# Attention and feed-forward layer on one core: the order of four engines written out in the source after the prologue, in place of the order of a rule-based planner

## The chip, the core and the metric

The kernel runs on one NeuronCore of a Trainium2 chip. The core has five engines with a queue each: TensorE (PE in the profile, its weight loads PEld), VectorE (DVE), ScalarE (ACT), GpSimd (POOL) and SyncE (SP), which here only issues transfers. Each engine works through its queue strictly in order, and the engines wait for one another through semaphores. The metric is the device time of one execution in microseconds (us): 689.67 us is the median of three runs of the kernel before (689.6 to 689.73).

## What is computed

The reference normalises an input `x` of 2048 rows by 640 columns, and adds three things: `x`, a multi-query attention with 32 heads of 20 columns each that share one key and one value head, and a feed-forward layer with 1728 hidden columns.

```python
q = (xn @ wq).reshape(B, S, 32, 20).transpose(0, 2, 1, 3)
k = xn @ wk                       # 2048 x 20, shared by all heads
v = xn @ wv                       # 2048 x 20
p = softmax(einsum("bhqd,bkd->bhqk", q, k) * 20 ** -0.5)
attn = einsum("bhqk,bkd->bhqd", p, v) ... @ wo
ffn = silu(xn @ w1) @ w2
out = x + attn + ffn
```

The bulk is the softmax: 32 heads x 2048 x 2048 exponentials.

## The kernel before, in words

**Tiling.** The queries are cut into four chunks of 512 and the heads into eight groups of four, which makes 32 groups; the keys into 16 tiles of 128. One score tile ("a head" below) is 128 keys x 512 queries of one head, and there are 32 x 16 x 4 = 2048 of them. A score matmul (`s_mm`, L1078) uses only 32 rows of the array, so matmuls of up to four different heads run at the same time in different rows; such a bundle is called a burst (`pe_set`, `joined`, L279). Each head fills one of PSUM's eight banks.

**Two ways for an exponential.** Most heads go to ScalarE: a set of two or three adjacent banks is read by one `exp` activation (L1166), and the result goes into slots of `Ebuf`; then one step of four matmuls per four heads multiplies with `v` (`make_pv_act`, L1201). The others go to VectorE in batches of four heads: `p1` (L1409) turns a score into the bit pattern of a bfloat16 power of two (one instruction per head, which also frees the bank), two shifts per batch make two more copies with other rounding (on GpSimd L1448, or on VectorE L1453), and three such matmul steps per batch, one per copy, form the weighted sum. A batch therefore costs TensorE two steps more than four heads on ScalarE do.

**Other work.** TensorE also runs the matmuls of `q`, of the hidden layer (`h`), of the output (`out`, and `y` for the last chunk), all through `col_mm` (L447). ScalarE has a `tanh` per hidden tile (L773), VectorE evicts all of these (L693, L776, L903, L919), copies each group's sums (L1250) and takes reciprocals (L851), and GpSimd normalises each group (L860). In some `out` and `y` steps the hidden matrix fills only half of the rows; such steps can be cut into single row matmuls (`row_mm`, L454) that ride in the free rows of a burst. The shifts and GpSimd's normalising (`op.port`) use a port that VectorE and GpSimd share; GpSimd waits by a semaphore for the last shift of VectorE that the plan put ahead (`calm`, L833), while VectorE's place relative to GpSimd is set by the planned order alone.

**What sets the order.** While the program is built, `build` plays through a schedule on the host (`Sched`, the main loop at the end of `build`). Each engine has a pool of operations, and rules choose the next one: `step_pe` (L1842) for TensorE, from the candidates of `pe_candidates` (L1730), and `step_other` (L1964) for the others by priority and earliest start. `plan` (L1084) chooses the banks of the next set: three adjacent ones or two. `dve_items` (L1362) chooses the head for VectorE, `dve_advance` (L1420) decides between GpSimd and VectorE for a shift, `take` (L1639) the bank of another job, `row_slice` (L1776) the row matmuls that fill a burst. The string `PLAN` varies the rules by stretch. Then `emit` (L2017) writes each engine's list out as its instruction stream with the semaphore waits that the data need. On the chip every engine's order is fixed; nothing is chosen at run time.

**Slots of Ebuf.** `e_slot` and `e_free` (L1119) give a set consecutive slots; a slot is free when all steps that use any part of the earlier set have been put into the order.

Of the kernel before, what the change touches and what calls it, by code (L numbers as in the profile page):

```python
# [15 lines left out]
D = 640  # L16
# [4 lines left out]
HG = 4  # L21
# [12 lines left out]
NJ = len(SHIFT)  # L34
# [77 lines left out]
def rule(n):  # L112
    return PLAN[n] if n < len(PLAN) else "a"
PACE = 1.0
ENDLEAD = 0.04
ENDFROM = 0.85

# [57 lines left out]
    return max(n / 2.4 + 3.0, 58.0)  # L175


class Job:


    def __init__(self, name, cost):
        self.name = name
        self.cost = cost
        self.bank = None
        self.mms = deque()
        self.consumers = []
        self.ready = None
        self.fixed = None
        self.head = None
        self.batch = None  # L190
        self.dyn = False
        self.issued = 0
        self.rest = {}
        self.burst = None
        self.row = None

    @property
    def done(self):
# [130 lines left out]
def build(nc, A_x, A_wq, A_wk, A_wv, A_wo, B_x, B_w1, B_w2, out, stack):  # L329
# [781 lines left out]
    def left_over(banks, gone):  # L1111

        left = set(banks).difference(gone)
        return sum(r <= left for r in RUN3)

    e_owner = [None] * NSLOT
    e_next = [0]

    def e_free(k):  # L1119
        return e_owner[k] is None or all(o is not None and o.done for o in e_users[e_owner[k]])  # L1120

    def e_slot(k):
        p = e_next[0] if e_next[0] + k <= NSLOT else 0
        return p if all(e_free(q) for q in range(p, p + k)) else None

    def make_s_act():
        n = att["n"]
        if n >= 2 and not exp_ops[n - 2].done:
            return None
        buf = plan(n)  # L1130
        if buf is None:
            return None
        items = next_items(len(buf), peek=True)
        if not items:
            return None
        buf = buf[:len(items)]
        pre = s_pre(items)
        if pre is None or not all(p.done for p in pre):
            return None
        es = e_slot(len(buf))  # L1140
        if es is None:
            return None

        def f(pe):
            ins = None
            for b, (g, kt, i) in zip(buf, items):
                ins = s_mm(pe, b, g, kt, i)
            return ins
        reads = [r for g in {it[0] for it in items} for r in q_res[g]] + [res("kT", kt) for kt in {it[1] for it in items}]
        wr = [sc.banks[b] for b in buf]  # L1150
        op = Op("pe", f, 216.0 + 4 * (len(items) - 1), pre=pre, reads=reads, writes=wr,
                mode="s", prio=0.0, name=f"S{n}", slots=frozenset(it[2] for it in items))
        op.run = buf

        def com(op, n=n, items=items, buf=buf, es=es):
            next_items(len(buf))
            e_next[0] = es + len(buf)
            for k in range(es, es + len(buf)):
                e_owner[k] = n
            att["n"] += 1  # L1160
            sc.free -= set(buf)
            w = len(items) * QW

            def ef(a):
                if len(buf) == 1 or buf[1] == buf[0] + 1:
                    return a.activation(Ebuf[:, es * QW:es * QW + w], ps[:, buf[0] * BANK:buf[0] * BANK + w], AF.Exp, scale=ESCALE)  # L1166
                src = ps[:, buf[0] * BANK:(buf[0] + 1) * BANK]
                return a.activation(Ebuf[:, es * QW:es * QW + w].rearrange("p (n q) -> p n q", q=QW),
                                    bass.AP(ps, src.offset, [list(src.ap[0]), [(buf[1] - buf[0]) * BANK, len(buf)], [1, QW]]), AF.Exp, scale=ESCALE)
            eo = act(ef, t_act(w) - 1.0, pre=[op], reads=[sc.banks[b] for b in buf], writes=[res("E", es + k) for k in range(len(buf))], prio=0.0,  # L1170
                     name=f"exp{n}")
            eo.on_commit = lambda op: sc.free.update(buf)
            exp_ops[n] = eo
            e_users[n] = []
            for j, (g, kt, i) in enumerate(items):
                d = pv_pend.setdefault((g, kt), {})
                d[i] = (es + j, eo, n)
                if len(d) == HG:
                    pv_queue[g].append(("a", kt, d))
                    po = make_pv_act(g, kt, d)  # L1180
                    for nn in {x[2] for x in d.values()}:
# [153 lines left out]
    def z_slot():  # L1335
        return next((k for k in range(min(ru.zcap, len(z_t))) if z_idle(k)), None)
# [80 lines left out]
    def pool_load():  # L1417
        return sc.t["pool"] - sc.t["pe"] + sum(o.occ for o in sc.pools["pool"])

    def dve_advance(job):  # L1420
# [14 lines left out]
        for j in range(1, NJ):  # L1435
            qk = XQ[j - 1]
            if qk is not None and len(s_last[j - 1]) == NW[j - 1] and len(xq_read[qk]) == DC + FC and all(o.done for o in xq_read[qk]):
                s_last[j - 1].append(sc.order["pe"][-1])
            wi = min(range(len(s_last[j - 1])), key=lambda k: -1 if s_last[j - 1][k] is None or k == NW[j - 1] and isinstance(s_last[j - 1][k], Op) else s_last[j - 1][k]["nth"])
            old = s_last[j - 1][wi]  # L1440
            s_last[j - 1][wi] = st
            lent = wi == NW[j - 1]
            t = xnT[:, 0:HG, qk * QW:(qk + 1) * QW] if lent else s_t[j - 1][wi][:, :]
            zin = z16.rearrange("p (h q) -> p h q", h=HG) if lent else z16
            r = res("s", j, wi)
            args = dict(pre=st["p1"] + ([idb] + [norm_op[n] for n in range(NT)] if old is None else [old] if isinstance(old, Op) else [old["pv"][j]]), reads=zr, writes=[r], name=f"s{j}")
            if j in POOL_J or pool_load() < ru.pj:
                op = pool(lambda v, t=t, j=j, zin=zin: v.tensor_scalar(t.bitcast(I16), zin, float(SHIFT[j]), 1.0, ALU.add, ALU.mult),  # L1448
                          POOL_SHIFT, POOL_END, prio=0.3, **args)
                op.port = True  # L1450
                op.gate = calm(op)
            else:
                op = dve(lambda v, t=t, j=j, zin=zin: v.tensor_scalar_add(t.bitcast(I16), zin, float(SHIFT[j])), t_dve(N, 4),  # L1453
                         prio=SPRIO - 0.01 * j, **args)
# [183 lines left out]

    def take(job, e):  # L1639
        b = job.fixed  # L1640
        if b is None:
# [175 lines left out]
    def xbanks():  # L1817
        return [b for b in sc.free if b in XBANKS] if pro else sc.free
# [100 lines left out]
    def fresh_u():  # L1919
        return att["pgroup"] < NGR and att["pgroup"] not in ubank  # L1920

    def commit_pe(e, op, what):
        if what[0] == "pv":
            if fresh_u():
                ok = [b for b in xbanks() if bank_at(b, "p") <= e + SLACK_B]
                b = min(ok, key=lambda b: (-left_over(sc.free, (b,)), -b)) if ok else min(xbanks(), key=bank_free_at)
# [51 lines left out]
    def finished():  # L1978
        return (att["pgroup"] >= NGR and not pro and not misc and not misc_front and cur_job[0] is None
                and all(not sc.pools[e] for e in sc.ENG))  # L1980

    idle = 0
    piece = 0
    while not finished():
# [7 lines left out]
        got = step_pe() if e == "pe" else step_other(e)  # L1992
        others = [sc.t[k] for k in sc.ENG if k != e]
        nxt = min(others)
        if got is None:
# [11 lines left out]
        idle = 0  # L2007
        if e == "pe":
            commit_pe(es, op, what)
        else:  # L2010
            sc.pools[e].remove(op)
            sc.commit(op, es)

    return sc, dma_sems, sem

# [158 lines left out]
```

## Time and profile before

| | |
|---|---|
| time, median of three runs | 689.67 us |
| span of the profiled execution | 688.3 us |
| TensorE busy, matmuls | 675.7 us (98%), 9821 |
| ScalarE busy | 666.4 us (97%), 728 instructions |
| VectorE busy | 591.3 us (86%), 1017 instructions |
| GpSimd busy | 581.7 us (85%), 349 instructions |
| transfers | 28.97 MB, mean 42 GB/s |

The profiled execution's span runs from its first to its last instruction; no separate time of that execution is given, so the 1.4 us between the span and the median are what lies around it. "Busy" is the union of the intervals in which instructions of the engine ran. Since matmuls overlap one another in the array and one activation overlaps the start of the next, a duration is longer than the distance from one start to the next; both are used below. A line "L1166" is a line of the kernel before.

### The profile page before, as it was taken

The numbers are of one execution on the slowest core, as the hardware profiler recorded it, in microseconds if no ns is written. First come the engines' busy times: TensorE is split into PE (matmuls) and PEld (weight loads), VectorE is DVE, ScalarE is ACT, GpSimd is POOL, SyncE is SP. The second block draws the span as 40 slices with busy tenths as digits, with TensorE's granted clock in tenths as the row PEclk, the third lists the DMA queues.
The fourth block names the chain that finished last, engine by engine and source line by source line (L and its number), as shares of the span: only waits on it lengthen the run. The fifth ranks groups of instructions, "written<-read, shape, count | busy, mean of one in ns | idle before, by whom it ended". The sixth has DMA issues, their size and how long they took to land.

```text
span 688.3 us, 22511 instructions
## 1 busy us (share of the span) xinstructions
PE 675.7 (98%) x9821; PEld 232.2 (34%) x9821; DVE 591.3 (86%) x1017; ACT 666.4 (97%) x728; POOL 581.7 (85%) x349
## 2 busy tenths in 40 slices
PE   8999999999999999999999999999999999999998
PEld 6432222222333333322323333332233333333345
DVE  7899988999989878798898897889999898987953
ACT  6999999999999999999999999999999999999992
POOL 6658899898988998899898889888889987879990
PEclk9999999999999999999999999999999999999999
DMA  8643220222221222422022222132222221223201
GB/s 226 190 160 42 19 23 14 35 34 25 23 29 12 32 38 29 72 36 30 9 22 30 29 31 33 26 37 61 31 22 20 21 27 23 32 20 70 23 7 41
DMA packets 34241, 28.97 MB, mean 42 GB/s; under 512 B 15486, under 2 KB 29662, under 8 KB 34142
## 3 DMA queue, kind: packets, MB, share of 16 engines
q1 hardware_dynamic: 33854, 27.20, 25.8%
q8 instruction: 77, 1.26, 0.8%
q10 hardware_dynamic: 288, 0.33, 0.1%
q14 instruction: 22, 0.18, 0.1%
HBM read 11.09 MB, written 2.62 MB: 20 GB/s over the span
## 4 chain that ended last, share of the span: by engine, by line
ACT 52%; PE 42%; DVE 3%; POOL 1%; DMA 0%; issue 0%; DVEq 0%; ACTq 0%
ACT sbt L1166 48%; PE psall L1201 14%; PE psall L1078 14%; PE psall L447 13%; ACT sbt L773 3%; DVE sbt L1409 2%; POOL sbt L1448 1%; PE psall L595 1%; PE psall L621 1%; DVE sbt L1453 0%; DMA sbt<-in_A_x_dram 0%; PE psall L999 0%; PE psall L1017 0%; ACT sbt L554 0%; DVE sbt L565 0%
## 5 line engine op out<-in xcount | busy, mean ns | idle before, releaser
L1166 ACT ACTIVATE sbt<-psall 128x1024 bf16<-128x1024 f32 (+1 forms) x656 | 640.0, 1138 | 3.2 <-PE psall L1078 3.0
L1448 POOL TENSOR_SCALAR sbt<-sbt 128x2048 int16<-128x2048 int16 x273 | 518.6, 1900 | 72.5 <-PE psall L1201 15.3
L1409 DVE TENSOR_SCALAR sbt<-psall 128x512 int16<-128x512 f32 x676 | 440.1, 685 | 63.1 <-PE psall L1078 58.0
L1078 PE MATMUL psall<-sbt 32*128 32x512 bf16 x2048 | 268.3, 384 | 3.3 <-ACT sbt L1166 2.0
L1201 PE MATMUL psall<-sbt 128*32 128x512 bf16 x3400 | 264.7, 384 | 1.9 <-POOL sbt L1448 0.6
L447 PE MATMUL psall<-sbt 128*32 128x320 bf16 (+2 forms) x3772 | 225.9, 332 | 2.1 <-DVE sbt L776 0.7
L1078 PEld LDWEIGHTS psall<-sbt 32*128 32x128 bf16 x2048 | 71.8, 91 | 236.9 <-ACT sbt L1166 174.1
L447 PEld LDWEIGHTS psall<-sbt 128*32 128x32 bf16 x3772 | 80.4, 95 | 85.5 <-issue 45.4
L1201 PEld LDWEIGHTS psall<-sbt 128*32 128x32 bf16 x3400 | 68.8, 94 | 115.5 <-issue 71.9
L1453 DVE TENSOR_SCALAR sbt<-sbt 128x2048 int16<-128x2048 int16 x65 | 47.6, 750 | 0.0
L860 POOL TENSOR_TENSOR sbt<-sbt 128x512 bf16<-128x512 f32 x30 | 38.3, 1277 | 4.9 <-DVE sbt L1453 2.7
L776 DVE SCALAR_TENSOR_TENSOR sbt<-sbt,psall 128x512 bf16<-128x512 bf16 x52 | 35.5, 682 | 3.8 <-ACT sbt L773 1.8
L773 ACT ACTIVATE sbt<-psall 128x512 bf16<-128x512 f32 x52 | 34.9, 671 | 0.2 <-PE psall L447 0.2
L454 PE MATMUL psall<-sbt 32*128 32x320 bf16 (+1 forms) x78 | 24.4, 313 | 0.0
L1250 DVE COPY sbt<-psall 128x512 f32<-128x512 f32 x31 | 21.2, 683 | 0.9 <-PE psall L1201 0.8
L919 DVE SCALAR_TENSOR_TENSOR sbt<-psall,sbt 128x320 f32<-128x320 f32 x8 | 3.9, 491 | 12.2 <-PE psall L447 7.0
L903 DVE SCALAR_TENSOR_TENSOR sbt<-psall,sbt 128x320 bf16<-128x320 f32 x24 | 11.6, 482 | 3.1 <-PE psall L447 1.7
L693 DVE TENSOR_SCALAR sbt<-psall 128x512 bf16<-128x512 f32 x20 | 13.5, 676 | 0.0
L572 POOL TENSOR_TENSOR sbt<-sbt 128x2 f32<-128x2 f32 x8 | 5.7, 710 | 8.5 <-DVE sbt L570 8.2
L1725 PE MATMUL psall<-sbt 128*32 128x256 bf16 (+1 forms) x188 | 11.1, 375 | 1.2 <-DVE sbt L487 1.2
L585 POOL TENSOR_SCALAR sbt<-sbt 128x640 bf16<-128x640 bf16 x12 | 10.4, 878 | 1.5 <-DVE sbt L577 1.5
L563 DVE BATCH_NORM_STATS2 sbt<-sbt 128x6 f32<-128x320 bf16 x14 | 6.6, 472 | 2.0 <-DMA sbt<-in_A_x_dram 2.0
(64 smaller groups left out, 118.3 us busy)
## 6 DMA issues: line engine op xcount, KB each, us to landing
sbt<-sbt SPq DMA_DIRECT2D x120, 64.0 KB, 3.8
sbt<-in_A_x_dram SPq DMA_DIRECT2D x28, 160.0 KB, 3.9
sbt<-sbt SPq DMA_DIRECT2D x213, 20.0 KB
out_dram<-sbt SPq DMA_DIRECT2D x14, 160.0 KB, 2.2
sbt<-in_B_w_dram SPq DMA_DIRECT2D x1, 2160.0 KB, 11.5
sbt<-in_B_w_dram SPq DMA_DIRECT2D x1, 2080.0 KB, 8.2
sbt<-sbt SPq DMA_DIRECT2D x75, 8.0 KB
sbt<-in_A_wq_dram SPq DMA_DIRECT2D x1, 800.0 KB, 6.7
```

Of the source, the lines that this page charges most:

```text
L447: ins = pe.matmul(ps[j * SLOT:(j + 1) * SLOT, b * BANK + off:b * BANK + off + n], w[:, j * SLOT:(j + 1) * SLOT], x, start=start, stop=stop ...
L454: return pe.matmul(ps[0:w.shape[-1], b * BANK:b * BANK + n], w[k], x[k], start=start, stop=stop, tile_position=(r * SLOT, 0))
L773: t = Op("act", lambda a: a.activation(t_buf[0:rows, ts, :], bk(job.bank, 0, QW, rows=rows), AF.Tanh, scale=0.5), t_act(512), ACT_END, pre ...
L776: u = Op("dve", lambda v: v.scalar_tensor_tensor(out=hT[par][0:rows, fk, :], in0=t_buf[0:rows, ts, :], scalar=1.0, in1=bk(job.bank, 0, QW, ...
L860: nm = pool(lambda e: e.tensor_tensor(oU[:, us, :], U_sb[:, us, :], Rrep, ALU.mult), 1356.0, POOL_END, pre=[uc] + lc + pack_op.get(divmod( ...
L1078: return pe.matmul(bk(b), kT_rep[i * SLOT:(i + 1) * SLOT, kt * P:(kt + 1) * P], qT[i * SLOT:(i + 1) * SLOT, g % NQ, :], start=True, stop=T ...
L1166: return a.activation(Ebuf[:, es * QW:es * QW + w], ps[:, buf[0] * BANK:buf[0] * BANK + w], AF.Exp, scale=ESCALE)
L1201: ins = pe.matmul(ps[i * SLOT:(i + 1) * SLOT, ub * BANK:ub * BANK + QW], lhsT, rhs, start=(first and k < HG), stop=(last and k >= len(lst) ...
L1250: return v.tensor_copy(U_sb[:, us, :], bk(ub))
L1409: p1 = Op("dve", lambda v: v.tensor_scalar(z16[:, i * QW:(i + 1) * QW], bk(job.bank), ZBIAS, 0.0, ALU.add, ALU.max), t_dve(QW) + 2.0, DVE_ ...
L1448: op = pool(lambda v, t=t, j=j, zin=zin: v.tensor_scalar(t.bitcast(I16), zin, float(SHIFT[j]), 1.0, ALU.add, ALU.mult), POOL_SHIFT, POOL_E ...
L1453: op = dve(lambda v, t=t, j=j, zin=zin: v.tensor_scalar_add(t.bitcast(I16), zin, float(SHIFT[j])), t_dve(N, 4), prio=SPRIO - 0.01 * j, **args)
```

## The change

Two strings are added. `ORDER` holds TensorE's order as tokens of three characters, 3046 of them; `OTHERS` holds the order of ScalarE, VectorE and GpSimd as one letter per operation, and under "port" the turns of GpSimd and VectorE on the shared port. Once TensorE's planned time has reached `HAND` (36 us), the prologue's jobs are done and no job is open, `follow` takes the next token in place of `step_pe`, and `follow_other` the next letter in place of `step_other`. SyncE's order stays with the rule. When the tokens run out, the rules go on.

A token `S20` is a set of two banks from bank 0 for ScalarE, `S14` a set of one bank, `D32` head 3 of the first open batch for VectorE into bank 2 (the first digit codes the batch, open or new, and the head), `E32` the same where the first of the batch's two shifts goes to VectorE instead of GpSimd, `a` and `d` a matmul step with `v` for heads of ScalarE or of VectorE, `n` the start of another job with its bank and `m` the next matmul step of that job. The small letter `s` (and `F`, `G`) starts a new burst where the capital would have joined the one before. There is no token for a single row matmul, and none for a filler.

The tokens and letters by count:

| | |
|---|---|
| sets for ScalarE: three banks, two banks, one bank | 69, 496, 56 (1255 heads) |
| heads for VectorE (D, E, F, G) | 705 |
| steps with `v`: a, d | 313, 518 |
| jobs begun: h, out, q, y | 54, 24, 18, 5 |
| further job steps m | 788 |
| ACT letters: exp, tanh | 621, 54 |
| DVE letters: p1, shifts, h, sums, out, q, y, other | 705, 116, 56, 30, 24, 18, 5, 3 |
| POOL letters: shifts, normalising | 234, 30 |

The rest of the diff: a slot of `Ebuf` becomes free as soon as the one step that reads it is in the order (`e_pv`); `make_s_act` takes the banks from the token, and for a token leaves out the rule that the exponential two sets before must be in the order; a job takes its bank from the token (`job.want`); the batch carries the choice of engine for its shift (`st["pool"]`).

```diff
+HAND = 36000.0
+ORDER = (
...
+OTHERS = {
+    "act": (
...
-    e_owner = [None] * NSLOT
+    e_pv = [FREE] * NSLOT
     def e_free(k):
-        return e_owner[k] is None or all(o is not None and o.done for o in e_users[e_owner[k]])
+        return e_pv[k] is not None and e_pv[k].done
...
-    def make_s_act():
+    def make_s_act(buf=None):
         n = att["n"]
-        if n >= 2 and not exp_ops[n - 2].done:
-            return None
-        buf = plan(n)
         if buf is None:
+            if n >= 2 and not exp_ops[n - 2].done:
+                return None
+            buf = plan(n)
+        if buf is None or not sc.free.issuperset(buf):
             return None
...
-            if j in POOL_J or pool_load() < ru.pj:
+            if j in POOL_J or st.get("pool", pool_load() < ru.pj):
...
+        if job.want is not None:
+            b = job.want
+            sc.free.remove(b)
...
+    def follow():
+        tok = ORDER[replay["at"]:replay["at"] + 3]
+        k, a, b = tok[0], tok[1], int(tok[2], 36)
+        if k in "sFG":
+            sc.pe_set = None
+            k = {"s": "S", "F": "D", "G": "E"}[k]
+        if k == "S":
+            op = make_s_act(tuple(range(b, b + int(a))))
+            what = ("s", None)
+        elif k in "DE":
...
+            dj.want = b
+            st["pool"] = k == "D"
+            op, what = dj.mms[0], ("dj", dj)
+        elif k in "ad":
...
+        elif k == "m":
+            op, what = cur_job[0].mms[0], ("mm", None)
+        elif k == "n":
...
+    def follow_other(e):
+        t = sc.t[e]
+        todo = OTHERS[e][replay[e]:replay[e] + 1]
+        if not todo:
+            return step_other(e)
...
+        for op in sc.pools[e]:
+            if sort_of(op) == todo:
+                if op.port and OTHERS["port"][replay["port"]] != e[0]:
+                    return None
+                es = sc.est(op)
+                return None if es is None else (es, op, todo)
+        return None
...
+        if e == "pe" and not replay["on"] and not replay["at"] and ORDER and sc.t["pe"] >= HAND and cur_job[0] is None and not pro:
+            replay["on"] = True
+        got = (follow() if replay["on"] else step_pe()) if e == "pe" else follow_other(e) if replay["on"] and e != "sp" else step_other(e)
```

More of the change, by code (lines that the diff above doesn't have):

```diff
@@ L175, in t_mm @@
     return max(n / 2.4 + 3.0, 58.0)
+FREE = SimpleNamespace(done=True)
 class Job:
@@ L195, in __init__ @@
         self.row = None
+        self.want = None
     @property
@@ L1158, in com @@
             for k in range(es, es + len(buf)):
-                e_owner[k] = n
+                e_pv[k] = None
             att["n"] += 1
@@ L1180, in com @@
                     po = make_pv_act(g, kt, d)
+                    for x in d.values():
+                        e_pv[x[0]] = po
                     for nn in {x[2] for x in d.values()}:
@@ L1640, in take @@
         b = job.fixed
-        if b is None:
+        if job.want is not None:
+            b = job.want
+            sc.free.remove(b)
+            if job.head is None:
+                job_hold[0] += 1
+        elif b is None:
             ok = [b for b in xbanks() if bank_at(b, job.ops[0].mode) <= e + SLACK_B]
@@ new lines, in build, with sort_of @@
+    kinds = {"p1": "p", "s1": "s", "s2": "s"}
+    def sort_of(op):
+        if op.name in kinds:
+            return kinds[op.name]
+        if op.name.startswith("Ucopy"):
+            return "u"
+        if op.name.startswith("exp"):
+            return "e"
+        if op.eng == "pool" and op.port:
+            return "n"
+        if op.job is not None and op.eng == "act":
+            return "t" if op.job.name[0] == "h" else "g"
+        if op.job is not None and op.eng == "dve" and op.name != "recip":
+            return op.job.name[0] if op.job.name[0] in "qhoy" else "g"
+        return None
@@ new lines, in follow_other @@
+    def follow_other(e):
[4 more added lines that the diff above has]
+        for op in sc.pools[e]:
+            k = sort_of(op)
+            if k is None:
+                es = sc.est(op)
+                if es is not None and es <= t:
+                    return es, op, None
+        for op in sc.pools[e]:
+            if sort_of(op) == todo:
+                if op.port and OTHERS["port"][replay["port"]] != e[0]:
+                    return None
+                es = sc.est(op)
+                return None if es is None else (es, op, todo)
+        return None
@@ L2009, in build @@
             commit_pe(es, op, what)
+            if replay["on"]:
+                replay["st"] = None
+                replay["at"] += 3
+                replay["on"] = replay["at"] < len(ORDER)
         else:
@@ L2012, in build @@
             sc.commit(op, es)
+            if what is not None:
+                replay[e] += 1
+                replay["port"] += op.port
     return sc, dma_sems, sem
```

139 lines of the change are left out of this document (137 added, 2 removed).

## The prediction

> **What bounds the kernel now.** I read the page first: the busy shares, and the slices of the span.
>
> ```profile
> span 688.3 us, 22511 instructions
> PE 675.7 (98%) x9821; PEld 232.2 (34%) x9821; DVE 591.3 (86%) x1017; ACT 666.4 (97%) x728; POOL 581.7 (85%) x349
> PE   8999999999999999999999999999999999999998
> DVE  7899988999989878798898897889999898987953
> ACT  6999999999999999999999999999999999999992
> POOL 6658899898988998899898889888889987879990
> PEclk9999999999999999999999999999999999999999
> ```
>
> Two engines are full over nearly the whole span, TensorE and ScalarE; the other two are at 85%. The clock is full everywhere, so no throttle enters. To tell the two full engines apart I cut off the prologue (to 37 us) and the finish (from 675 us), and ask what ScalarE waited for in between.
>
> ```profile
> 37.00:675.00 638.00, 631.44 (x9073) 205.88 (x9076) 555.68 (x911) 636.27 (x689) 559.86 (x308) 1.00 0.24 32
> ACT sbt L1166 <- PE psall L1078: 1.4, 3, 0.6
> ACT 52%; PE 42%; DVE 3%; POOL 1%; DMA 0%; issue 0%; DVEq 0%; ACTq 0%
> ```
>
> The columns of the first row are the stretch, its length and busy time of PE, PEld, DVE, ACT and POOL. ScalarE works 636.3 of 638 us and waits 1.4 us for scores. It **is** the bound of this stretch: whatever shortens it must take work off ScalarE. But the chain of waits (third row) is 42% TensorE, and TensorE is at 631.4: a change that gives TensorE more than a few us would move the bound there. So both sums are needed.
>
> **Prices.** For ScalarE the durations by shape, and the chain, whose pieces go from start to start:
>
> ```profile
> L1166 ACT ACTIVATE sbt<-psall 128x1024 bf16<-128x1024 f32 x594 | 563.5, 1100 | 2.6 <-PE psall L1078 2.5
> L1166 ACT ACTIVATE sbt<-psall 128x1536 bf16<-128x1536 f32 x61 | 89.7, 1512 | 0.6 <-PE psall L1078 0.6
> L773 ACT ACTIVATE sbt<-psall 128x512 bf16<-128x512 f32 x52 | 34.9, 671 | 0.2 <-PE psall L447 0.2
> ...
> 95.46 2.75 ACT sbt L1166 x3
> 98.21 0.49 ACT sbt L773
> ```
>
> A set of two banks takes a step of 2.75/3 = 0.917 us; one bank more costs 1.512 - 1.100 = 0.412, so three banks step 1.329. Only one exponential of one bank ran before, and it has no row of its own. From below it is 0.917 - 0.412 = 0.505, or the 0.49 of the `tanh` on the same 512 columns; from above the 0.671 of that `tanh` as a lone duration. I take 0.505, as the `tanh` stands between exponentials as the new sets will. [...]
>
> For TensorE, from the chain:
>
> ```profile
> 655.30 0.32 PE psall L1078 x3
> 656.01 0.22 PE psall L1201 x4
> 675.59 2.44 PE psall L447 x72
> ```
>
> A step with `v` is 0.22; an output step is four matmuls of 320 columns, so 2.44/18 = 0.136; a step of `h` or `q` has 512 columns as the `v` step has and gets 0.22. A burst streams 512 columns too: 0.22, and the other 0.10 of its 0.32 is the change of array mode, which is paid at the way in and at the way out.
>
> **What the change removes, adds and moves.** I count tokens, and compare with the list of operations that the planner of before puts out after the prologue, up to the same 1960 heads (1255 + 705).
>
> *ScalarE.* Before: 568 sets of two and 52 of three, 568 x 0.917 + 52 x 1.329 = 590 us, with 1292 heads. After: 496, 69 and 56 of one, 454.8 + 91.7 + 28.3 = 574.8 us, with 1255. The tanhs stay. So **-15.1 us**; with one bank at 0.49 it is -16.0, at 0.671 it is -5.8. The work leaves ScalarE because 37 heads more go to VectorE (705 for 668). Over the whole kernel that is nine batches: 169 before, 178 after.
>
> *TensorE.* Bursts fall from 692 to 601, since more of them carry four heads (203; in all of before 87, and 67 more that a row matmul filled up), among them those with two sets. Mode changes fall from 1241 to 1137. Against that the new batches raise the steps with `v` from 818 to 831. And the row matmuls that rode in bursts for nothing are gone:
>
> ```profile
> L454 PE MATMUL psall<-sbt 32*128 32x320 bf16 x70 | 21.3, 305 | 0.0
> ```
>
> Their 70 matmuls (and 8 wide ones) come back as whole steps, 456 for 432 of `out`, 73 for 67 of `y` and 360 for 358 of `h` and `q`. Their cover was the burst; without it they cost 30 x 0.136 + 2 x 0.22 = 4.5 us. The 11 fillers go. Sum: -91 x 0.22 - 104 x 0.10 + 13 x 0.22 + 4.5 - 11 x 0.22 = **-25.5 us**. If the mode change were wholly hidden in the new bursts or twice as dear this would be -15 to -36; either way TensorE falls at least as far as ScalarE, and ScalarE stays ahead.
>
> *VectorE and GpSimd.* Here the change gives back.
>
> ```profile
> L1409 DVE TENSOR_SCALAR sbt<-psall 128x512 int16<-128x512 f32 x676 | 440.1, 685 | 63.1 <-PE psall L1078 58.0
> L1453 DVE TENSOR_SCALAR sbt<-sbt 128x2048 int16<-128x2048 int16 x65 | 47.6, 750 | 0.0
> L1448 POOL TENSOR_SCALAR sbt<-sbt 128x2048 int16<-128x2048 int16 x273 | 518.6, 1900 | 72.5 <-PE psall L1201 15.3
> L860 POOL TENSOR_TENSOR sbt<-sbt 128x512 bf16<-128x512 f32 x30 | 38.3, 1277 | 4.9 <-DVE sbt L1453 2.7
> ...
> 266.47 1.28 DVE L1453 TENSOR_SCALAR sbt<-sbt 128x2048 int16<-128x2048 int16 x2
> 267.67 4.87 DVE L1409 TENSOR_SCALAR sbt<-psall 128x512 int16<-128x512 f32 x8
> 259.53 0.48 DVE L903 SCALAR_TENSOR_TENSOR sbt<-psall,sbt 128x320 bf16<-128x320 f32 x1
> L851 DVE RECIPROCAL sbt<-sbt 128x16 f32<-128x16 f32 x30 | 7.3, 242 | 0.1
> ```
>
> Dense, a `p1` steps (4.87 - 0.69)/7 = 0.60 us and a shift 1.28 - 0.69 = 0.59, less than their busy means (0.65, 0.73). The order holds 705 p1, 116 shifts, 104 other wide evictions at the p1's price, 29 of 320 columns at 0.48 and 30 reciprocals: 423 + 68 + 62 + 14 + 7 = 574 us, next to ScalarE's 574.8 + 54 x 0.49 = 601.3. VectorE comes to 95% of the bound. GpSimd hands 51 shifts to VectorE and gets 18 for the nine new batches, 33 x 1.90 = 63 us less; it was not on the path. On the shared port stand 234 x 1.90 + 30 x 1.28 + 68 = 551 us, less than ScalarE's sum. VectorE's new work, 36 x 0.65 + 51 x 0.73 = 61 us at busy means, is hidden in its idle time of 638 - 556 = 82 us.
>
> *Rest.* SyncE's rule, the transfers, the prologue and the finish stay. After the tokens, 38 heads and three `y` jobs follow by the old rules, as many heads as the planner of before has left at that point. The earlier release of `Ebuf` slots costs no instruction.
>
> **The gaps.** Sums hide local unevenness. Cutting both orders into pieces of twenty sets (about 19 us) and adding in each piece only the fullest engine's sum, at the prices above, gives 604.7 for 601.3 of ScalarE alone after, and 633.7 for 631.6 before: 1.3 us more of gaps. With pieces of ten it is 611.8 and 636.6: 5.5 more. Buffers hold several sets, so I stay near the lower one, 2 us.
>
> **Sum.** 688.3 - 15.1 + 2 = 675.2 us of span, and with the 1.4 us between span and median **676.5 us**.
>
> **The rivals.**
>
> *VectorE becomes the bound, through the port (slower).* VectorE's shifts share a port with GpSimd, and 65 of them become 116.
>
> ```profile
> L1453 DVE TENSOR_SCALAR sbt<-sbt x65: 629/685/1569, 57.2 to 662.8; 128x2048 int16<-128x2048 int16 x65
> DVE sbt L1409 <- PE psall L1078: 57.5, 162, 1.9
> ```
>
> The longest shift took 0.94 us above the shortest; the mean loss against the dense step is 0.73 - 0.59 = 0.14. VectorE's room beside ScalarE is 601 - 574 = 27 us, so from 0.23 us lost per shift it decides. At 0.40, it is 574 + 46 = 620, which is 19 us above ScalarE's 601: 688.3 - 15.1 + 19 + 1.4 = 693.6 us, slower by 4. A late `p1` holds a bank, behind it wait the rest of VectorE's queue and the next burst into that bank, and so ScalarE. Against it: GpSimd's shifts all last 1.90 us, the losses so far are small, and the port turns are part of the order. [...]
>
> *Gaps of strict order eat the gain (no change).* ScalarE waited 1.4 us before. With four engines at 80 to 100% in one fixed order, a wait of 0.024 us at each of the 621 sets would be 15 us: 689.7. For it: p1 waited 57.5 us for scores, so TensorE does come late. Against it: the order before was as strict, with TensorE and ScalarE both at 99%, and TensorE now gets ten us more room.
>
> *Half the gain.* The one-bank sets at 0.671 (-5.8), or gaps as in pieces of ten or a little more: 683 us.
>
> That the order isn't followed is no rival: it is built into each queue.
>
> **Chances and range.** The forecast 0.68, half the gain 0.14, no change 0.05, the port 0.13. Changes of up to 0.2% (1.4 us) can't be told from none. Faster is 0.68 + 0.14 = 0.82, same 0.05, slower 0.13. Low end: ScalarE's -16.0 with no gaps, and 2 us off a finish that now starts with another `y` mix, 688.3 - 18.0 + 1.4 = 671.5. The high end takes in half the gain and part of the no-change case, 687; the port lies outside.
>
> **What would show it.** Right: ScalarE's busy time in the stretch falls by about 15 us and it still waits under 5 us; about 660 exponentials with 56 of 512 columns more, each a step of 0.5 us; p1 712 times; shifts on VectorE about 116 at a mean under 0.8 us; the finish after the last exponential stays at 13 us, as the end of before has it:
>
> ```profile
> 659.67 15.44 ACT L1166 ACTIVATE sbt<-psall 128x1024 bf16<-128x1024 f32 x13
> 684.35 1.34 DVE L967 SCALAR_TENSOR_TENSOR sbt<-psall,sbt 128x512 bf16<-128x512 f32 x2 [0.30 <-PE psall L447]
> ```
>
> Wrong: ScalarE idle for 10 us or more, with the waits on L1078 and behind those on L1409 or L1453; shifts on VectorE with a mean of 1 us; one-bank sets that step 0.67.

## The result, and the profile after

The kernel with the written order takes 681.3 us (median of 4 runs, 680.93 to 682.5) against 689.68 us before: ratio 0.9882, 95% interval 0.9868 to 0.9896. It is faster by 8.4 us, where 13.2 were forecast. The profiled execution spans 679.4 us for 688.3, so 8.9 us less. Runs that have both numbers show 1.8 us between time and span (681.22 and 679.4 here, 689.96 and 688.2 for before), not the 1.4 us worked out above; by that the profiled execution of before took some 0.4 us more than its median, and most of the difference between 8.9 and 8.4 is this.

The page of the changed kernel, the lines that answer to those of before (L1258 is the old L1166, L1168 the old L1078, L1295 the old L1201, L1503 the p1 of L1409, L1547 and L1542 the shifts of L1453 and L1448):

```profile
span 679.4 us, 22817 instructions
PE 666.0 (98%) x9898; PEld 240.8 (35%) x9901; DVE 632.2 (93%) x1102; ACT 654.4 (96%) x728; POOL 514.1 (76%) x314
...
DVE  7899999999998999899999999999999899999943
ACT  6999999999998999999999999999999899999992
...
PEclk9999999999998999999999999999999899999999
...
PE 63%; ACT 20%; DVE 13%; POOL 3%; issue 1%; DMA 0%; POOLq 0%; ACTq 0%
...
L1542 POOL TENSOR_SCALAR sbt<-sbt 128x2048 int16<-128x2048 int16 x238 | 451.5, 1897 | 112.3 <-PE psall L1295 40.9
L1503 DVE TENSOR_SCALAR sbt<-psall 128x512 int16<-128x512 f32 x712 | 454.6, 682 | 20.3 <-PE psall L1168 15.2
L1547 DVE TENSOR_SCALAR sbt<-sbt 128x2048 int16<-128x2048 int16 x118 | 80.8, 710 | 0.6 <-PE psall L1295 0.5
```

VectorE fills its idle time (its wait for scores falls from 58 to 15 us), GpSimd has more of it (76% busy for 85%), and the chain of waits moves from ScalarE (52%, now 20%) to TensorE. The new thing stands in the row of the clock: two slices of 8 where there was none. In the same two slices ScalarE has its only 8s.

The groups of ScalarE by shape:

```profile
L1258 ACT ACTIVATE sbt<-psall 128x1024 bf16<-128x1024 f32 x520 | 494.9, 1049 | 6.6 <-PE psall L1168 5.7
L1258 ACT ACTIVATE sbt<-psall 128x1536 bf16<-128x1536 f32 x80 | 116.1, 1485 | 0.2
L1258 ACT ACTIVATE sbt<-psall 128x512 bf16<-128x512 f32 x56 | 34.8, 632 | 0.3
```

At the steps of the prediction that is 520 x 0.917 + 80 x 1.329 + 56 x 0.505 = 611.4 us for 626.3 before (594, 61 and 1): 14.9 us off ScalarE's sum, as forecast. But the time between the starts of consecutive activations, taken from the trace and set against the plain step of each shape (0.917, 1.344, 0.49), shows what is lost between them. (The shortest steps in the trace are 0.904, 1.330 and 0.477; with these both kernels lose 9.0 us more, and the difference between them stays as it is.)

| kernel | lost between activations, 37 us to the last | of it in 200-220 us | of it in 520-540 us |
|---|---|---|---|
| before | 4.9 us | -0.1 | -0.1 |
| changed | 12.1 us | 2.5 | 2.5 |

So 7.2 us more gaps, and 14.9 - 7.2 = 7.7; the finish after the last exponential shrinks from 13.2 to 12.6 us. That leaves 0.6 of the 8.9 us of span. Over two thirds of the new gaps, 5.2 us, lie in two places, those with the low clock.

Here is the first of them, in stretches of one microsecond (busy time of PE, PEld, DVE, ACT, POOL with the number of instructions, then the clock):

```profile
205.00:206.00 1.00, 0.87 (x8) 0.19 (x5) 1.00 (x3) 1.00 (x2) 0.68 (x1) 1.00 0.43 63
207.00:208.00 1.00, 0.65 (x11) 0.20 (x7) 1.00 (x3) 1.00 (x2) 0.69 (x1) 1.00 0.07 16
209.00:210.00 1.00, 0.52 (x8) 0.25 (x12) 1.00 (x3) 1.00 (x2) 0.00 (x0) 0.72 0.08 21
210.00:211.00 1.00, 1.00 (x16) 0.20 (x8) 1.00 (x3) 0.21 (x1) 0.81 (x1) 0.50 0.08 21
211.00:212.00 1.00, 1.00 (x12) 0.24 (x12) 0.23 (x2) 0.04 (x1) 1.00 (x1) 0.50 0.16 41
214.00:215.00 1.00, 1.00 (x22) 0.34 (x22) 0.70 (x2) 1.00 (x2) 0.92 (x2) 1.00 0.00 0
```

From 205 us TensorE runs 7 to 11 matmuls a microsecond instead of 22; it is waiting for VectorE, which is full. At 209.4 us its clock falls to half for 3.4 us. From then on TensorE is late, and ScalarE, full until 210.2, stands still. The timelines of the two engines over the same place:

```profile
208.46 0.40 PE L1295 MATMUL psall<-sbt 128*32 128x512 bf16 x4
209.49 1.90 PE L1295 MATMUL psall<-sbt 128*32 128x512 bf16 x16 [0.63 <-DVE sbt L1547]
211.31 0.61 PE L1168 MATMUL psall<-sbt 32*128 32x512 bf16 x4
...
211.96 1.02 ACT L1258 ACTIVATE sbt<-psall 128x1024 bf16<-128x1024 f32 x1 [1.75 <-PE psall L1168]
```

Sixteen matmuls take 1.90 us (20 of the same take 1.26 at full clock, in a row shown below); ScalarE waits 1.75 us for the score behind them. At 530.3 us the same happens again. All four executions have a mean clock below one, 0.992 to 0.997, where before had 0.999 to 1.000.

### The profile page after: what moved, and what is told of

The parts are those of the page before. It is cut to its first block, busy times and chain, and to the rows that moved or that the text cites. A ratio compares the mean times of both kernels' runs of the same rounds, so it can differ in the third digit from the quotient of the medians.

```text
span 679.4 us, 22817 instructions
## 1 busy us (share of the span) xinstructions
PE 666.0 (98%) x9898; PEld 240.8 (35%) x9901; DVE 632.2 (93%) x1102; ACT 654.4 (96%) x728; POOL 514.1 (76%) x314
## 4 chain that ended last, share of the span: by engine, by line
PE 63%; ACT 20%; DVE 13%; POOL 3%; issue 1%; DMA 0%; POOLq 0%; ACTq 0%
PE psall L1295 21%; PE psall L1168 20%; PE psall L537 20%; ACT sbt L1258 18%; DVE sbt L1503 7%; POOL sbt L1542 3%; ACT sbt L863 1%; DVE sbt L1547 1%; DVE sbt L866 1%; DVE sbt L653 1%; DVE sbt L697 0%; DVE sbt L655 0%; PE psall L711 0%; DVE sbt L783 0%; DVE sbt L1344 0%
## 5 line engine op out<-in xcount | busy, mean ns | idle before, releaser
L1258 ACT ACTIVATE sbt<-psall 128x1024 bf16<-128x1024 f32 (+2 forms) x656 | 624.4, 1067 | 7.1 <-PE psall L1168 5.7
L1542 POOL TENSOR_SCALAR sbt<-sbt 128x2048 int16<-128x2048 int16 x238 | 451.5, 1897 | 112.3 <-PE psall L1295 40.9
L1503 DVE TENSOR_SCALAR sbt<-psall 128x512 int16<-128x512 f32 x712 | 454.6, 682 | 20.3 <-PE psall L1168 15.2
L1295 PE MATMUL psall<-sbt 128*32 128x512 bf16 x3472 | 273.6, 386 | 2.1 <-DVE sbt L1547 0.8
L1168 PE MATMUL psall<-sbt 32*128 32x512 bf16 x2048 | 255.8, 386 | 4.4 <-ACT sbt L1258 1.0
L537 PE MATMUL psall<-sbt 128*32 128x320 bf16 (+3 forms) x3900 | 218.9, 332 | 0.4 <-DVE sbt L1503 0.2
L1168 PEld LDWEIGHTS psall<-sbt 32*128 32x128 bf16 x2048 | 69.3, 91 | 225.6 <-ACT sbt L1258 125.6
L537 PEld LDWEIGHTS psall<-sbt 128*32 128x32 bf16 (+1 forms) x3900 | 84.2, 96 | 86.8 <-issue 46.6
L1295 PEld LDWEIGHTS psall<-sbt 128*32 128x32 bf16 x3472 | 72.8, 95 | 109.2 <-issue 70.6
L1547 DVE TENSOR_SCALAR sbt<-sbt 128x2048 int16<-128x2048 int16 x118 | 80.8, 710 | 0.6 <-PE psall L1295 0.5
L685 PE MATMUL psall<-sbt 128*128 128x128 bf16 x80 | 6.9, 220 | 1.5 <-DVE sbt L678 1.5
```

What stands on the lines that cost most here:

```text
L537: ins = pe.matmul(ps[j * SLOT:(j + 1) * SLOT, b * BANK + off:b * BANK + off + n], w[:, j * SLOT:(j + 1) * SLOT], x, start=start, stop=stop ...
L1168: return pe.matmul(bk(b), kT_rep[i * SLOT:(i + 1) * SLOT, kt * P:(kt + 1) * P], qT[i * SLOT:(i + 1) * SLOT, g % NQ, :], start=True, stop=T ...
L1295: ins = pe.matmul(ps[i * SLOT:(i + 1) * SLOT, ub * BANK:ub * BANK + QW], lhsT, rhs, start=(first and k < HG), stop=(last and k >= len(lst) ...
L1503: p1 = Op("dve", lambda v: v.tensor_scalar(z16[:, i * QW:(i + 1) * QW], bk(job.bank), ZBIAS, 0.0, ALU.add, ALU.max), t_dve(QW) + 2.0, DVE_ ...
```

## The experiments

All times are medians; the kernel of before ran next to each, with medians between 689.6 and 689.8 us.

| kernel | time | ratio to before, 95% interval |
|---|---|---|
| changed | 681.3 | 0.9882 (0.9868 to 0.9896) |
| fill_a: changed, 16 fillers | 678.92 | 0.9843 (0.983 to 0.9857) |
| fill_c: changed, 27 fillers | 679.17 | 0.9848 (0.9834 to 0.9861) |
| late_norm: fill_a, one turn moved | 679.37 | 0.9852 (0.9836 to 0.9868) |
| thin_fill_before | 689.62 | 1.0 (0.9991 to 1.0008) |
| exp_cut_before | 688.45 | 0.9983 (0.9974 to 0.9992) |
| out_cut_before | 688.88 | 0.9988 (0.9978 to 0.9997) |
| both_cut_before | 685.17 | 0.9933 (0.9919 to 0.9948) |
| exp_cut_fill | 677.29 | 0.9822 (0.9807 to 0.9836) |
| out_cut_fill | 676.39 | 0.9807 (0.9792 to 0.9821) |
| p1_cut_fill | 677.02 | 0.9818 (0.9802 to 0.9835) |
| both_cut_fill | 672.84 | 0.9755 (0.9738 to 0.9771) |
| all_cut_fill | 668.85 | 0.9697 (0.9682 to 0.9711) |

### Is the missing gain the clock?

The planner of before has a rule that puts in fillers, matmuls of zeros, where TensorE is thin; the written order replaced the rule and holds none. The first kernel brings the rule back on top of the written order:

```diff
+    def warm(got):
+        t = sc.t["pe"]
+        if streamed() >= 0.7:
+            return got
+        gap = 999.0 if got is None else got[0] - t
+        if gap > (330.0 if sc.pe_mode == "s" else 100.0):
+            op = filler(gap)
+            e = sc.est(op) if op is not None else None
+            if e is not None and e <= t + 40:
+                return e, op, ("fill", None)
+        return got
...
-        got = (follow() if replay["on"] else step_pe()) if e == "pe" else ...
+        got = (warm(follow()) if replay["on"] else step_pe()) if e == "pe" else ...
```

> The changed kernel with 16 fillers put into its order after the prologue, where TensorE would wait and has streamed under 0.7 of its last 2.4 us (matmuls of zeros added to an open sum; the planner of before had 11 such, the written order none). Theory A (the gap between forecast and result is the clock: the two half-clock stretches of 3.4 us near 209 and 530 us follow from thin TensorE work there): the granted clock stays at 1.000, ScalarE's long waits at 210 and 531 us shrink from about 2 us each to under 0.7 us each, and the time falls by 2.5 to 5 us from 681.3, to 676.5 to 679. Theory B (the waits there are VectorE's and GpSimd's own lateness on the shared port, and the clock only follows): the clock may stay up but the time stays within 1 us of 681.3. Theory C (fillers don't hold the clock): the half-clock stretches are still there, 681 or more.

It took 678.92 us, 2.4 us less than the changed kernel, with a clock of 1.000 in all five runs. The first place again in the kernel with 16 fillers, by stretches (columns as above) and by its timeline:

```profile
206.00:208.00 2.00, 1.98 (x34) 0.70 (x38) 2.00 (x3) 2.00 (x3) 1.08 (x1) 1.00 0.11 26
208.00:210.00 2.00, 1.65 (x31) 0.60 (x27) 2.00 (x4) 1.73 (x2) 0.19 (x1) 1.00 0.09 23
210.00:212.00 2.00, 2.00 (x35) 0.55 (x28) 2.00 (x4) 1.51 (x3) 1.89 (x1) 1.00 0.12 29
```

```profile
209.45 1.26 PE L1295 MATMUL psall<-sbt 128*32 128x512 bf16 x20
209.56 1.02 ACT L1258 ACTIVATE sbt<-psall 128x1024 bf16<-128x1024 f32 x1 [0.27 <-PE psall L1168]
211.08 5.29 ACT L1258 ACTIVATE sbt<-psall 128x1024 bf16<-128x1024 f32 x5 [0.49 <-PE psall L1168]
```

ScalarE's wait of 1.75 us has become 0.27 and 0.49. Its lost time falls from 12.1 to 9.1 us in all (1.1 in 200-220 us, 0.9 in 520-540 us). Theory A holds for the mechanism: hold the clock, and 2.4 us come back. Its size, 2.4 us, is just under the 2.5 to 5 that it expected, since the waits at those places do not vanish; about 1 us at each stays, which is the part of theory B that is true.

> The same with 27 fillers: the share below which one is put in is 0.6, and a planned wait of 20 ns (within a mode) or 150 ns (with a change of mode) is enough. Theory A: the clock is 1.000 as well and the time is within 1 us of the kernel with 16 fillers, since the extra ones lie in stretches that kept the clock without them. Theory B: 681 or more, by up to 2 us, since each extra filler of 0.11 or 0.22 us takes TensorE's time. Theory C: half-clock stretches remain.

The kernel differs from fill_a in three numbers (0.6 for 0.7, 150 for 330, 20 for 100).

It took 679.17 us with the clock at 1.000, within theory A. The 27 fillers are no better than 16: at 196.7 us this kernel has a new gap of 1.5 us on ScalarE that the other has not, which was not followed further.

If fillers hold the clock, the old order should lose it without them. The edit leaves that order as it was and makes its 11 late fillers 32 columns wide:

```diff
-                ins = pe.matmul(ps[i * SLOT:(i + 1) * SLOT, ub * BANK:ub * BANK + n], zero_t[:, 0:SLOT], zero_t[:, 0:n],
+                ins = pe.matmul(ps[i * SLOT:(i + 1) * SLOT, ub * BANK:ub * BANK + k], zero_t[:, 0:SLOT], zero_t[:, 0:k],
```

with `k = 32` after the prologue.

> The kernel of before, its order unchanged, with the 11 fillers after the prologue cut from 512 or 256 columns to 32 each. Theory A: the load of TensorE falls at the fillers' places (about 68, 195, 333, 474 and 535 us), at least one half-clock stretch of 3.4 us appears there, and the time rises by 1 to 2.5 us for each, 690.5 to 697. Theory B and C (fillers don't matter to the clock): granted clock 1.000 and 689.7 within 0.5.

It took 689.62 us, ratio 1.0, and no half-clock stretch. So this expectation of theory A fell: the old order did not need its fillers. The edit also left the thinnest stretch of that order as it was, as no filler stands there. What lost the clock is not only that fillers went; the new order makes TensorE thinner in places than the old one is anywhere. The first two rows are of the changed kernel, the 3.41 us that end where the clock falls (209.43 and 530.28 us); the third is the stretch just ahead of the first; the row after them is the thinnest of before (the count in brackets includes matmuls that reach in from ahead):

```profile
206.02:209.43 3.41, 2.23 (x21) 0.58 (x21) 3.41 (x5) 3.41 (x4) 1.56 (x1) 1.00 0.11 27
526.87:530.28 3.41, 2.33 (x25) 0.65 (x24) 3.40 (x6) 3.41 (x4) 3.12 (x3) 1.00 0.10 24
202.60:206.02 3.42, 2.92 (x29) 0.81 (x26) 3.42 (x7) 3.42 (x5) 3.00 (x2) 1.00 0.69 75
```

```profile
109.30:112.71 3.41, 2.50 (x29) 0.64 (x29) 2.96 (x5) 3.41 (x5) 3.25 (x3) 1.00 0.00 0
```

TensorE is busy for 2.23 and 2.33 us where the clock was lost, and for 2.50 us or more in every such stretch of before, which kept it. With the 16 fillers no stretch of this length has less than 2.9. The number of matmuls does not tell the two apart: 19 and 25 start in the first two rows, 25 each in the last two.

The rest of the edits needs no run of its own: with an empty order string, the changed source builds the same program as before, instruction for instruction.

### Which engine bounds?

The prediction read ScalarE as the bound of before. A cut of work tells: each `exp` from the 40th set on leaves out its last 32 columns, in the old order and in the new one with fillers. The output is not the reference's, as these columns of the softmax are stale.

```diff
-   return a.activation(Ebuf[:, es * QW:es * QW + w], ps[:, buf[0] * BANK:buf[0] * BANK + w], AF.Exp, scale=ESCALE)
+   c = w - 32 if n >= 40 else w
+   return a.activation(Ebuf[:, es * QW:es * QW + c], ps[:, buf[0] * BANK:buf[0] * BANK + c], AF.Exp, scale=ESCALE)
```

> The kernel of before with its order unchanged; each exponential on ScalarE from the 40th set on leaves out its last 32 columns (616 of 656 sets, a column 0.412/512 us, so 616 x 0.0258 = 15.9 us off ScalarE's queue). Theory A (ScalarE alone is the bound of the stretch, as the prediction read it): the time falls by 12 to 16 us, to 674 to 678. Theory D (TensorE's queue is as full as ScalarE's and bounds as well): it falls by under 5 us, 685 to 690.

688.45 us: 16 us off ScalarE's queue are worth 1.2. The cut itself took effect: the shortest distance between the starts of two exponentials of two banks falls from 0.904 to 0.876 us, but the mean only from 0.924 to 0.923. The chain of waits says why, before and with the cut:

```profile
ACT 52%; PE 42%; DVE 3%; POOL 1%; DMA 0%; issue 0%; DVEq 0%; ACTq 0%
```

```profile
PE 84%; DVE 8%; POOL 4%; ACT 1%; issue 1%; DMA 0%; DVEq 0%; POOLq 0%; ACTq 0%
```

As soon as ScalarE is a little faster, most of the chain runs through TensorE. ScalarE alone was not the bound; theory D.

> The same cut (616 sets, 15.9 us off ScalarE's queue) in the written order with 16 fillers. Theory A (ScalarE is still ahead, by the 20 us that the sums leave TensorE): 678.9 falls by 12 to 16 us, to 663 to 667. Theory D (in a strict order every engine waits for the slowest of the moment, and the four are close): it falls by 3 to 9 us, 670 to 676, since TensorE's and VectorE's sums come to lie within 2% of ScalarE's.

677.29 us, 1.6 us less than fill_a: less than the 3 that even theory D expected at least.

The next edit takes work off TensorE: the matmuls of `out` and `y` stream 256 of 320 columns, so that the last 64 columns of each half of the output are not computed.

```diff
-            f = (e1 - e0, hT[par][:, fk, i * P:(i + 1) * P], w2_sb[:, fk, e0:e1])
+            f = (e1 - e0 - 64, hT[par][:, fk, i * P:(i + 1) * P], w2_sb[:, fk, e0:e1 - 64])
...
-            f = (e1 - e0, oT[0:n, qc % 2, c, i * P:(i + 1) * P], wo_sb[0:n, c, e0:e1])
+            f = (e1 - e0 - 64, oT[0:n, qc % 2, c, i * P:(i + 1) * P], wo_sb[0:n, c, e0:e1 - 64])
```

> The written order with 16 fillers; every matmul of the output steps (out and y, 580 steps) streams 256 columns of 320, 580 x 0.136 x 64/320 = 15.8 us off TensorE's queue. Theory A (TensorE has room): the time falls by under 2 us from 678.9. Theory D: by 4 to 9 us, 670 to 675.

676.39 us, 2.5 less than fill_a: more than theory A allowed and less than theory D did, so neither is met.

> The kernel of before, order unchanged, output steps (549 whole ones of out and y) streaming 256 of 320 columns: 549 x 0.0272 = 14.9 us off TensorE's queue alone. Theory A2 (in before it is TensorE, not ScalarE, that sets the pace, since ScalarE's cut gave 1.2 us): 10 us or more off, under 680. Theory D (the two pace each other, neither has room): under 4 us off, 686 to 689.

688.88 us, 0.9 less than before. TensorE is no lone bound either, and the chain of this run is the mirror image of the one with ScalarE's cut:

```profile
ACT 73%; PE 17%; DVE 6%; POOL 3%; issue 1%; DMA 0%; POOLq 0%; DVEq 0%; ACTq 0%
```

And work off VectorE, in the new order: the last 32 columns of each p1 from the 13th batch on are left out.

```diff
-        p1 = Op("dve", lambda v: v.tensor_scalar(z16[:, i * QW:(i + 1) * QW], bk(job.bank), ZBIAS, 0.0, ALU.add, ALU.max),
+        k = QW - 32 if len(batches) > 12 else QW
+        p1 = Op("dve", lambda v: v.tensor_scalar(z16[:, i * QW:i * QW + k], bk(job.bank, 0, k), ZBIAS, 0.0, ALU.add, ALU.max),
```

> The written order with 16 fillers; from the 13th batch on VectorE's p1 leaves out the last 32 of its 512 columns (about 664 of 712, each 0.033 us by 1.04 ns a column, 22 us off VectorE's queue). Theory A (VectorE has 27 us of room): the time falls by under 2 us. The rival of the prediction (VectorE is the bound, by itself or through the port): it falls by 8 us or more. Theory D: 2 to 6 us.

677.02 us, 1.9 less than fill_a; the mean p1 falls from 683 to 652 ns, which over the 664 of 712 that were cut is 33 ns each, 1.04 ns a column. By the letter it is theory A's "under 2 us", and too near theory D's lower end of 2 to tell the two apart. VectorE is not the bound that the prediction's rival named, since that asked for 8. GpSimd, at 76%, and the transfers were not cut.

Cuts together, made of the same edits:

> The kernel of before with both cuts, 15.9 us off ScalarE's and 14.9 us off TensorE's queue, the order unchanged. Theory D: the two cuts together give far more than the sum of the single ones, 10 to 15 us off, 675 to 680, about what the written order does by moving the sums of both engines. Theory E (the order itself, not the sums, sets the time; a search is needed to use the room): under 5 us off, 685 or more.

685.17 us, 4.6 less than its neighbours of before. It is more than the 1.2 and 0.9 of the single cuts together, as theory D says, but a third of the 15 us that both queues lost, as theory E says.

> The written order with 16 fillers and both cuts, ScalarE's 15.9 us and TensorE's 15.8 us. If in the written order those two bind alone, 678.9 falls by 10 us or more, under 669. If VectorE (574 us of work by the prediction's sum, now level with ScalarE's 601 less 16) binds as the third, it falls by 3 to 7 us, 672 to 676.

672.84 us, 6.1 less than fill_a, within the 3 to 7 that were expected if VectorE binds as the third.

> The same with p1 cut as well (22 us off VectorE). If VectorE is the third that binds, this falls by 10 us or more from 678.9, under 669, and by 5 us or more from the kernel with both cuts. If the order of the operations itself is the limit, by under 2 us from the kernel with both cuts.

668.85 us, 10.1 less than fill_a and 4.0 less than with both cuts, where 5 or more were expected of VectorE as the third that binds and under 2 if the order alone is the limit. So VectorE's cut is worth 4.0 us once the other two are lighter, for 1.9 alone, and still 10 us is all that 16 to 22 us off each of three queues give. The chain of that kernel:

```profile
PE 67%; DVE 16%; ACT 13%; POOL 3%; issue 1%; DMA 0%; POOLq 0%; DVEq 0%; ACTq 0%
```

Two thirds of it run through TensorE, which had lost an estimated 15.8 us, and a third through the other three. A reading that fits, but that no run singles out: in a fixed order each of the short waits has its own engine behind it, and a uniform cut removes only those that stand behind the engine that was cut.

### Does the shared port cost?

The rival of the prediction has a place in the trace. In the changed kernel VectorE's longest shift, 1.76 us, begins at 207.7 us, under GpSimd's normalising of a group. The shifts of the changed kernel, and GpSimd over that place:

```profile
L1547 DVE TENSOR_SCALAR sbt<-sbt x118: 628/683/1761, 60.1 to 650.0; 128x2048 int16<-128x2048 int16 x118
```

```profile
207.31 1.56 POOL L950 TENSOR_TENSOR sbt<-sbt 128x512 bf16<-128x512 f32 x1 [1.63 <-DMA sbt<-sbt]
```

GpSimd waited 1.63 us for a transfer and started late. VectorE's second shift, begun at 207.67 us, ended at 209.43 us, 0.56 us after GpSimd's normalising; the median of the 118 shifts is 0.68 us. So it was with the longest shift of before, 1.57 us: begun at 650.16 us under GpSimd's shifts, it ended at 651.73 us, 0.55 us after those (651.18). It is by such delays that the shared port shows in the traces. The last kernel, on top of fill_a, lets the three shifts go first, by moving one letter of the port's string behind three others:

```diff
-pppddpppdddpppdpd
+pppddppdddppppdpd
```

> The written order with fillers; at one place (near 207 us) GpSimd's normalising of a group goes behind VectorE's three shifts instead of ahead of them (one turn of the port order moved by three; the filler rule then puts in 14 instead of 16, four fewer right there). The prediction's rival (the shared port costs at this place): VectorE's longest shift there falls from 1.70 to under 0.8 us, ScalarE's waits of 0.3 and 0.5 us at 209 to 211 vanish, 678.9 falls by 0.5 to 1.5. Against it: the group's normalised rows come 1.5 to 2 us later, the output steps that fill TensorE after 211 us start later, and the time stays or rises by up to 1.5; with fewer fillers the half-clock stretch may come back, for another 1 to 2.

It took 679.37 us against 678.92; the intervals of the two overlap, so neither is shown faster. At this place the mechanism is as the rival says. The three shifts there take 1.89 us instead of the 2.90 of fill_a (the fillers differ too, 14 here for 16):

```profile
207.12 1.89 DVE L1547 TENSOR_SCALAR sbt<-sbt 128x2048 int16<-128x2048 int16 x3
209.10 1.28 POOL L950 TENSOR_TENSOR sbt<-sbt 128x512 bf16<-128x512 f32 x1 [3.36 <-DVE sbt L1547]
```

```profile
207.05 2.90 DVE L1547 TENSOR_SCALAR sbt<-sbt 128x2048 int16<-128x2048 int16 x3
```

The first fence is of the kernel with the turn moved, the second of fill_a. ScalarE's lost time at 209 to 211 us is gone, but two gaps of 0.49 and 0.54 us show up at 216 to 218 us. The trace of the kernel with the turn moved shows the port there once more: GpSimd's own three shifts start 0.4 us later than in fill_a (210.11 us), VectorE comes to its next shift 0.9 us sooner, still under the last of them, and this shift takes 2.08 us, for 0.79 in fill_a:

```profile
210.47 5.85 POOL L1542 TENSOR_SCALAR sbt<-sbt 128x2048 int16<-128x2048 int16 x3
214.78 2.08 DVE L1547 TENSOR_SCALAR sbt<-sbt 128x2048 int16<-128x2048 int16 x1
```

So this run moved the collision by 7 us and did not remove it (lost in 200-220 us: 1.1 us with fill_a, 1.4 here). What the place would be worth without any collision, it does not show.

**The kernel that beats both** is the changed one with 16 fillers: 678.92 us, interval 0.983 to 0.9857 against 0.9868 to 0.9896 of the changed kernel alone.

## Why the prediction was right, and where it was not

*ScalarE's sum, right.* 14.9 us off for a forecast of 15.1; 712 heads on VectorE and 118 shifts there as counted; the one-bank set, whose price had to be bounded, steps 0.476 to 0.493 us from start to start, where it does not wait (half of the 56), nearer the `tanh` row's 0.49 than the 0.505 taken and far from 0.671. The finish kept its 13 us within 0.6.

*The gaps, mis-sized.* This is the step that failed in the sum: "Buffers hold several sets, so I stay near the lower one, 2 us." Measured were 7.2. Of these 5.2 lie in the two places where the clock drops, and 2.0 elsewhere; without the drops, with fillers, the gaps are 9.1 - 4.9 = 4.2 us, inside the 1.3 to 5.5 that the two cuttings had given.

*The clock, missed.* The prediction wrote "The clock is full everywhere, so no throttle enters" of the old trace and carried it over; and it booked "The 11 fillers go" as a saving of 2.4 us of TensorE. It asked what a filler costs and not what it covers. That cover, as thin_fill_before shows, was not needed in the old order; it was needed in the new one, whose two places, 24 and 27 us behind the last scores of the first and the third query chunk, have nothing but scores and steps with `v` to run (from 192 to 213 and from 516 to 532 us TensorE has no step of another job; in before the longest such stretch is 8 us), and wait for a full VectorE.

*The bound, half right.* "It is the bound of this stretch: whatever shortens it must take work off ScalarE" is not how this kernel behaves. 15.9 us off ScalarE alone gave 1.2, and 15 us off both ScalarE and TensorE in the old order gave 4.6. The prediction did take both sums, and the change lowers both, but it turned ScalarE's sum into time one for one. Its step "either way TensorE falls at least as far as ScalarE, and ScalarE stays ahead" did not hold either: the chain of the changed kernel is 63% TensorE and 20% ScalarE. Its counts for TensorE hold (601 bursts and 1137 changes of mode stand in the tokens), and so does the price of a change: from one step with `v` to the next it is 0.216 us, from a burst to such a step or back 0.32, so 0.10 each way. But of the 25.5 us TensorE's busy time shows 9.7, 675.7 to 666.0, and it is 98% busy as before; whether the rest went into bursts whose heads come late, no run separates.

That the changed kernel still got 8.4 of 15 us, and 10.7 with its clock held, where the old order with lighter queues got 4.6, suggests that the order has its share, as it was fitted to the lighter queues. It is not shown: the cuts took 14.9 us off TensorE and the change was to take 25.5, and how much is the order's and how much the sums' share was not separated further. So it is in part luck that the time lies as near the forecast as it does: the sum that gave it prices one engine alone, and no run bears that out.

*Two sums.* 675.2 + 1.4 is 676.6, not 676.5, and the low end, 688.3 - 18.0 + 1.4, is 671.7, not 671.5; neither matters here.

*The rivals.* Strict order eating the whole gain did not happen, half the gain came nearest in size (683 us), by one of its two conditions: gaps "as in pieces of ten or a little more", 7.2 us for 5.5, though 3.0 of them (12.1 - 9.1) go with the clock; the other, one-bank sets at 0.671, did not come. The port's rival was real at one place, where a shift took 1 us too long, and not in the sum: mean loss per shift against the dense 0.59 is 0.68 - 0.59 = 0.09 us by busy time (80.8 us for 118), below the 0.14 of before and the 0.23 from which it would decide.

## What to carry to other kernels

When two engines are both at 98% or more of a stretch in a fixed order, neither need be the bound: here a cut of 15 us on one of them bought 0.9 or 1.2 us, a cut on both 4.6, and the same cut on both in the new order 6.1. Before an idle-looking piece of work (a filler, a spare matmul) is dropped, ask what it holds up, and after every rearrangement look at the row of the clock, since a place of a few microseconds where TensorE waits on a full neighbour (busy for 2.23 of the 3.41 us ahead of the first drop) was enough to halve it here. Price the gaps of a hand-written order by cutting it into stretches of two sizes; in this one case the middle of the two, 3.4 us, was nearer the 4.2 measured with the clock held than the lower end was.

## What the runs showed of the hardware

The clock fell though TensorE never stood still for long: its longest single wait ahead of the first drop was 0.63 us. The two half-clock stretches of the profiled execution last 3.41 us each, from 209.43 and from 530.28 us, at a granted clock of 0.50. Where the limit lies was not measured: in the 3.41 us just ahead of the drops TensorE was busy for 2.23 and 2.33 us, and the thinnest stretch of that length in before, with 2.50, kept the clock. The profiled execution has two drops, and the other three have mean clocks of 0.992 to 0.997; since one drop takes 3.4 x 0.5 / 679 = 0.25% of the mean, these are one to three drops: an estimate that says that the same order does not lose the clock equally often every time.

Exponentials run closer together than their durations suggest: in the changed kernel at the shortest 0.90 us from start to start for two banks, 1.33 for three and 0.48 for one, at mean durations of 1.05, 1.49 and 0.63 us.
